# Seven quarter products for the mixture's first layer, in an attention and feed-forward kernel on one Trainium2 core

## The chip, the cores and the metric

The kernel runs on one core of a Trainium2 chip. Its time is that of the device in microseconds, a median over runs. A profile is one execution with an instruction trace.

## The reference

Three layers follow one another on 1152 tokens of 512 features. An attention (2 sequences, 8 heads, 576 tokens, 64 features a head) adds a softmax over pooled groups of four tokens and a local one in a band. Its output x goes through a feed-forward layer of 2048 hidden units, and that through a mixture of four experts of 1024 hidden units each, every expert on every token:

```python
def _moe_ref(x, w_in, w_out, s, b):
    h = x @ w_in
    r = np.maximum(h, 0.0)
    return (s * (r * r) + b) @ w_out

def _moe2_ref(x, domain_probs, w1, w2):
    p = domain_probs / (domain_probs.sum(-1, keepdims=True) + 1e-09)
    out = np.zeros_like(x)
    for e in range(4):
        h = np.maximum(x @ w1[e], 0.0)
        out += p[:, e:e + 1] * (h @ w2[e])
    return out
```

## The kernel before

Each float32 operand of a large product is split into two float32r parts, hi and lo, and a product is made in three passes: hi hi, hi lo, lo hi (`PAIRS`, line 209 in `products`). Activations are stored with features on the partitions: `xs[0]`, `xs[1]` are the hi and lo parts of x, [128, 4, 1152], and `acc` is the float32 sum of a layer's output, in the mixture seen as tokens by features (`acc_t`).

The hidden units are cut into blocks of 512: blocks 0 to 3 are the feed-forward layer, blocks 4 to 11 the mixture, two for each expert. The weights of a block come in four quarters of [128, 1024] (two of the first, two of the second matrix), loaded by `load_next` through SyncE's queue into two rotating `raw` buffers and made ready by `prep` in small steps: for the mixture a ScalarE cast (hi, L174) and a VectorE subtraction (lo, L178). The steps wait in a list, `side`; `side_step` takes one, and the plan calls it between products. The ready parts lie in the pools `wp`, `wx` and `wy`, four places for a half of a first matrix and four for a half of a second.

In the feed-forward layer `moe1_l1` makes 128 hidden units for a group of tokens with 12 products (four 128-row terms by three passes) and then square, scale and split on ScalarE and VectorE (L623 to L636); `moe1_l2` makes 128 output features and adds them to `acc` on VectorE (L651), in the last block also the hi and lo parts of the mixture's x (L653, L654). Groups are of 384 tokens in blocks 1 to 3. In the mixture `moe2_l1` makes 128 hidden units for a part of the tokens: part 0 has 640 tokens, as two pieces of 320 beside each other in two PSUM banks, part 1 has 512. Relu on ScalarE (L680) and a subtraction on VectorE (L681) give hi and lo. `moe2_l2` makes a tile of 128 tokens by 512 features with 12 products and adds it, weighted, on VectorE (L704). PSUM has eight banks: three in `psm`, five in `psx`, handed out by `mm_bank`.

After the attention the order is written as a plan of (time, step) that is sorted: the first layer of a stage stands beside the second layer of a stage before. The feed-forward's last second-layer steps stand beside the mixture's first steps. The plan's order is the order in which instructions are named; a scheduler in the build lays down each engine's queue, by priority in that order among the instructions whose inputs it takes to be there.

## Time and profile before

| | us |
|---|---|
| median of 3 runs | 727.75 (727.34 to 728.23) |
| span of the profiled execution | 727.1 |
| mean granted TensorE clock | 0.969 |
| TensorE busy | 714.3 |
| VectorE busy | 330.9 |
| ScalarE busy | 282.0 |
| GpSimd (POOL) busy | 54.1 |

The span runs from the first to the last instruction; the median is 0.65 us above it. Busy times are shares of the span, and an engine's own waits are not in them. Matmuls are pipelined, so the row of a group gives the length of one from its start to its modelled end, and the distance between two starts is what a product costs in a stream.

### The profile page before, as it was taken

How to read it: one execution, taken by the hardware profiler on the slowest of the kernel's cores; microseconds unless marked ns; L12 is line 12 of the kernel's file. 1: busy time of each engine (PE TensorE's matmuls, PEld its weight loads, DVE VectorE, ACT ScalarE, POOL GpSimd, SP SyncE). 2: the span in 40 equal slices, each digit the busy share in tenths (PEclk: the TensorE clock that was granted, in tenths of full speed). 3: DMA queues.
4: the chain of work that ended last, by engine and by line, in shares of the span. 5: the costliest groups of instructions: out<-in, count | busy, mean ns of one | idle time of the engine just before them, and what ended most of it. 6: DMA issues, size and time to landing. Idle time of an engine off the chain costs nothing.

```text
span 727.1 us, 10493 instructions
## 1 busy us (share of the span) xinstructions
PE 714.3 (98%) x4248; PEld 635.3 (87%) x4248; DVE 330.9 (46%) x573; ACT 282.0 (39%) x662; POOL 54.1 (7%) x62
## 2 busy tenths in 40 slices
PE   6999999999999999999999999999999999999997
PEld 3687888889999999999898898898988988988886
DVE  1468986678893432554213324333333243232222
ACT  2456867668975565733323113122122121120110
POOL 3235244120000000000000000000000000000000
PEclk7559999999999999999999999999999999999999
DMA  6446625533440010211101103003112021000012
GB/s 160 129 112 166 146 42 103 151 103 113 133 145 30 2 57 1 87 30 58 40 20 59 58 1 87 29 1 87 30 57 59 1 60 56 1 1 0 1 44 87
DMA packets 54545, 46.35 MB, mean 64 GB/s; under 512 B 32608, under 2 KB 43104, under 8 KB 54496
## 3 DMA queue, kind: packets, MB, share of 16 engines
q1 hardware_dynamic: 54496, 45.67, 22.9%
q8 instruction: 33, 0.54, 0.3%
q14 instruction: 16, 0.13, 0.1%
HBM read 43.31 MB, written 2.36 MB: 63 GB/s over the span
## 4 chain that ended last, share of the span: by engine, by line
PE 96%; DVE 1%; ACT 1%; SPq 1%; DMA 1%; POOL 0%; issue 0%
PE psx L209 47%; PE psm L209 36%; PE psa L473 3%; PE psa L551 2%; PE psa L485 2%; PE psa L523 2%; PE psa L245 1%; PE psa L544 1%; DMA v<-in_v_dram 1%; ACT pl L459 1%; PE psa L383 1%; PE psa L401 1%; PE psa L464 0%; SPq L320 0%; SPq L332 0%; DVE pl L502 0%
## 5 line engine op out<-in xcount | busy, mean ns | idle before, releaser
L209 PE MATMUL psx<-x,w 128*128 128x320 f32 (+2 forms) x960 | 187.8, 335 | 0.0
L209 PEld LDWEIGHTS psx<-x,w 128*128 128x128 f32 x960 | 161.8, 188 | 11.0
L209 PE MATMUL psm<-x,w 128*128 128x320 f32 (+3 forms) x816 | 159.0, 330 | 0.0
L209 PEld LDWEIGHTS psm<-x,w 128*128 128x128 f32 x816 | 134.1, 189 | 9.4 <-issue 2.3
L209 PE MATMUL psx<-w,h 128*128 128x512 f32 x528 | 126.7, 390 | 0.0
L209 PEld LDWEIGHTS psx<-w,h 128*128 128x128 f32 x528 | 98.4, 188 | 20.0
L680 ACT ACTIVATE h<-psx 128x320 fp32r<-128x320 f32 (+1 forms) x61 | 28.0, 489 | 143.5 <-PE psx L209 143.5
L209 PE MATMUL psm<-w,h 128*128 128x512 f32 x336 | 80.4, 390 | 0.0
L209 PEld LDWEIGHTS psm<-w,h 128*128 128x128 f32 x336 | 62.6, 188 | 12.6
L681 DVE SCALAR_TENSOR_TENSOR h<-psx,h 128x320 fp32r<-128x320 f32 (+1 forms) x61 | 32.3, 553 | 89.4 <-ACT h L680 89.4
L178 DVE TENSOR_TENSOR w<-raw,w 128x1024 fp32r<-128x1024 f32 x32 | 39.1, 1223 | 53.1 <-ACT w L174 53.1
L209 PE MATMUL psx<-h,w 128*128 128x384 f32 (+1 forms) x336 | 61.2, 330 | 0.0
L209 PEld LDWEIGHTS psx<-h,w 128*128 128x128 f32 x336 | 57.5, 188 | 0.0
L174 ACT CAST w<-raw 128x1024 fp32r<-128x1024 f32 x32 | 33.7, 1052 | 60.4 <-PE psx L209 35.6
L209 PE MATMUL psm<-h,w 128*128 128x384 f32 (+2 forms) x288 | 51.5, 320 | 0.0
L704 DVE SCALAR_TENSOR_TENSOR acc<-psx,pr,acc 128x512 f32<-128x512 f32 x39 | 29.3, 750 | 47.5 <-PE psx L209 47.2
L680 ACT ACTIVATE h<-psm 128x320 fp32r<-128x320 f32 (+1 forms) x35 | 16.4, 491 | 88.3 <-PE psm L209 88.3
L209 PEld LDWEIGHTS psm<-h,w 128*128 128x128 f32 x288 | 44.7, 188 | 2.7 <-issue 1.9
L681 DVE SCALAR_TENSOR_TENSOR h<-psm,h 128x320 fp32r<-128x320 f32 (+1 forms) x35 | 18.8, 556 | 55.0 <-ACT h L680 55.0
L704 DVE SCALAR_TENSOR_TENSOR acc<-psm,pr,acc 128x512 f32<-128x512 f32 x24 | 18.0, 751 | 29.2 <-PE psm L209 29.0
L636 DVE TENSOR_TENSOR h<-r,h 128x384 fp32r<-128x384 f32 x36 | 20.0, 555 | 19.7 <-ACT h L635 19.6
L634 ACT ACTIVATE r<-r,b_sb,s_sb 128x384 f32<-128x384 f32 x36 | 25.6, 712 | 0.9
(83 smaller groups left out, 681.4 us busy)
## 6 DMA issues: line engine op xcount, KB each, us to landing
raw<-in_moe_w_dram SPq DMA_DIRECT2D x32, 512.0 KB
raw<-in_moe_w_in_dram SPq DMA_DIRECT2D x8, 1024.0 KB
raw<-in_moe_w_out_dram SPq DMA_DIRECT2D x8, 1024.0 KB
kn<-in_k_dram SPq DMA_DIRECT2D x16, 144.0 KB
v<-in_v_dram SPq DMA_DIRECT2D x8, 288.0 KB
out_dram<-acc SPq DMA_DIRECT2D x9, 256.0 KB
qn<-in_q_dram SPq DMA_DIRECT2D x16, 80.0 KB
vn<-in_v_dram SPq DMA_DIRECT2D x16, 72.0 KB
```

The source lines that it names most:

```text
L174: nc.scalar.copy(parts[0], st["f"] if n < n_moe1 else raw[n, which, half])
L178: nc.vector.tensor_tensor(out=parts[1], in0=f, in1=f32(parts[0]), op=ALU.subtract)
L209: nc.tensor.matmul(o, stat(ps, kk), mov(pm, kk, i), start=c == 0, stop=c == len(terms) - 1)
L473: nc.tensor.matmul(ps[0][:, t * W : t * W + W], qz[:, t].rearrange("p a q -> p (a q)"), kT[:, k0 : k0 + W], start=False, stop=t == m - 1,)
L485: nc.tensor.matmul(pooled[a], qd[o, :], kd[o, :], start=True, stop=True)
L523: nc.tensor.transpose(ps[:W, n : n + width], x, ident[:width, :width])
L551: nc.tensor.matmul(ps[o, t * TQ : t * TQ + TQ], vn[:, t, a], pT[:, i : i + TQ], start=True, stop=True,)
L634: nc.scalar.activation(out=r, in_=r, func=ACTF.Identity, bias=b_sb, scale=s_sb)
L636: nc.vector.tensor_tensor(out=h[1], in0=r, in1=f32(h[0]), op=ALU.subtract)
L680: nc.scalar.activation(out=h[0][:, o : o + m], in_=ps, func=ACTF.Relu)
L681: nc.vector.scalar_tensor_tensor(out=h[1][:, o : o + m], in0=ps, scalar=0.0, in1=f32(h[0][:, o : o + m]), op0=ALU.max, op1=ALU.subtract,)
L704: nc.vector.scalar_tensor_tensor(out=a, in0=ps, scalar=p_e, in1=a, op0=ALU.mult, op1=ALU.add)
```

## The change

The mixture's first layer is computed by the scheme of seven products. A half of a block (256 hidden units) is a 2 by 2 matrix of quarters A11 to A22 (128 hidden units by 256 features), and a part of the tokens a 2 by 2 matrix B11 to B22 (256 features by half of the part's tokens). Seven products of quarters and of sums of quarters (S1 to S4 of the weights, T1 to T4 of x), with six matmuls each, give the four quarters of the hidden units. `step0` to `step3` hold them: three PSUM banks, a, b and c, are summed into by up to three products, and ScalarE copies (`copy`) and VectorE additions (`add`) take what lies in a bank between two of them.

The sums of x are made once, in `x_sums`, on VectorE and ScalarE. The sums of a weight quarter are made by four GpSimd additions (`total` in `prep2`) and split with the quarter itself in three `piece`s of 512, 256 and 1024 elements a partition. Part 0 stays 640 tokens, as halves of 320, part 1 512 as halves of 256; block 3's groups are cut likewise (320, 320, 256, 256). T1's hi and lo parts lie in place of x's own second half of features 0 to 255, which `moe1_l2` therefore no longer writes.

The mixture has a pool of its own, `m2`, opened after the feed-forward's plan has been run through and its pools closed; its tiles wait for the tiles that lay in the same place (`reuse_waits="tile"`). The mixture's first weights are loaded from there on. It holds two places for the sums of a half's first matrix, three for a half's second matrix, two raw buffers and sixteen h tiles. The mixture's second layer uses `psm` alone, the first `psx`. Comments that the change takes out are left away here.

```diff
@@ -61,9 +61,11 @@
 
     const = ctx.enter_context(tc.tile_pool(name="const", bufs=1))
     big = ctx.enter_context(tc.tile_pool(name="big", bufs=1))
-    wp = ctx.enter_context(tc.tile_pool(name="wp", bufs=1))
-    rawp = ctx.enter_context(tc.tile_pool(name="raw", bufs=2))
-    hp = ctx.enter_context(tc.tile_pool(name="hp", bufs=1))
+    m1ctx = ExitStack()
+    wp0 = m1ctx.enter_context(tc.tile_pool(name="wp0", bufs=1))
+    rawp = m1ctx.enter_context(tc.tile_pool(name="raw", bufs=2))
+    hp = m1ctx.enter_context(tc.tile_pool(name="hp", bufs=1))
+    wp1 = m1ctx.enter_context(tc.tile_pool(name="wp1", bufs=1))
     psm = ctx.enter_context(tc.tile_pool(name="psm", bufs=3, space=bass.MemoryType.PSUM))
...
@@ -92,7 +94,7 @@
     pools = {}
 
     def load_next():
-        if not stream:
+        if not stream or (stream[0][0] >= n_moe1 and "m2" not in pools):
...
-        t = rawp.tile([P, 2048], dt, tag="raw", name="raw")[:, : 1024 * m]
+        if n < n_moe1:
+            t = rawp.tile([P, 2048], dt, tag="raw", name="raw")
+        else:
+            t = pools["m2"].tile([P, 1024], dt, tag="raw2", name="raw2", bufs=2)
         nc.sync.dma_start(out=t.rearrange("p (a b) -> p a b", a=src.shape[1]), in_=src)
...
     def prep(n, which, half):
-        """One quarter made ready for the tensor engine, as small steps."""
+
+        if n >= n_moe1:
+            return prep2(n, which, half)
         i = (2 * n + half) % 4
         if i < 3 - which:
-            pool, nb = wp, 3 - which
+            pool, nb = (wp1 if which else wp0), 3 - which
         else:
...
@@ -171,23 +178,102 @@
             )
 
         def high():
-            nc.scalar.copy(parts[0], st["f"] if n < n_moe1 else raw[n, which, half])
+            nc.scalar.copy(parts[0], st["f"])
 
         def low():
-            f = st["f"] if n < n_moe1 else raw[n, which, half]
-            nc.vector.tensor_tensor(out=parts[1], in0=f, in1=f32(parts[0]), op=ALU.subtract)
+            nc.vector.tensor_tensor(
+                out=parts[1], in0=st["f"], in1=f32(parts[0]), op=ALU.subtract
+            )
             load_next()
             ready.add((n, which, half))
 
...
         nonlocal tail
-        if n < n_moe1:
-            steps = [magnitude] + tail[:1] + [clamp] + tail[1:] + [join, sign]
-            tail = [high, low]
-        else:
-            steps = tail + [high, low]
-            tail = []
+        steps = [magnitude] + tail[:1] + [clamp] + tail[1:] + [join, sign]
+        tail = [high, low]
         return steps
...
+    SLOT = {"A11": 0, "A12": 1, "A22": 2, "S1": 3, "S2": 4, "S3": 5, "S4": 6}
+
+    def prep2(n, which, half):
+        m2 = pools["m2"]
+        cols = 1024 if which else 7 * 256
+        parts = [
+            m2.tile([P, cols], F32R, tag=f"v{which}{c}", name=f"v{which}{c}", bufs=2 + which)
+            for c in range(2)
+        ]
+        wt[n, which, half] = parts
+
+        def done():
+            load_next()
+            ready.add((n, which, half))
+
+        if which:
+
+            def high():
+                nc.scalar.copy(parts[0], raw[n, which, half])
+
+            def low():
+                nc.vector.tensor_tensor(
+                    out=parts[1], in0=raw[n, which, half], in1=f32(parts[0]), op=ALU.subtract
+                )
+                done()
+
+            return [high, low]
+
+        sw = m2.tile([P, 4, 2, P], F32, tag="sw", name="sw", bufs=1)
+
+        def quarter(name):
+
+            w = raw[n, which, half].rearrange("p (k f) -> p k f", k=KD)
+            i, k = int(name[1]) - 1, int(name[2]) - 1
+            return w[:, 2 * k : 2 * k + 2, i * P : i * P + P]
+
+        def operand(name):
+            return quarter(name) if name[0] == "A" else sw[:, int(name[1]) - 1]
+
+        def total(out, x, y, op):
+            nc.gpsimd.tensor_tensor(out=operand(out), in0=operand(x), in1=operand(y), op=op)
+
+        def piece(i, c):
+            if i == 0:
+                src, cols = raw[n, which, half].rearrange("p (k f) -> p k f", k=KD)[:, :, :P], (0, 512)
+            elif i == 1:
+                src, cols = quarter("A22"), (512, 768)
+            else:
+                src, cols = sw.rearrange("p s k f -> p (s k) f"), (768, 1792)
+            out, hi = (
+                t[:, cols[0] : cols[1]].rearrange("p (k f) -> p k f", f=P)
+                for t in (parts[c], f32(parts[0]))
+            )
+            if c == 0:
+                nc.scalar.copy(out, src)
+                return
+            nc.vector.tensor_tensor(out=out, in0=src, in1=hi, op=ALU.subtract)
+            if i == 2:
+                done()
+
+        return [
+            lambda: total("S1", "A21", "A22", ALU.add),
+            lambda: piece(0, 0),
+            lambda: total("S2", "S1", "A11", ALU.subtract),
+            lambda: piece(0, 1),
+            lambda: total("S3", "A11", "A21", ALU.subtract),
+            lambda: piece(1, 0),
+            lambda: total("S4", "A12", "S2", ALU.subtract),
+            lambda: piece(1, 1),
+            lambda: piece(2, 0),
+            lambda: piece(2, 1),
+        ]
+
+    def s_ap(n, half, part, name, kk):
+        while (n, 0, half) not in ready:
+            side_step()
+        c0 = SLOT[name] * 256 + kk * P
+        return wt[n, 0, half][part][:, c0 : c0 + P]
...
-    # the queries of two heads in the blocks of a diagonal: one product makes both heads' scores
-    qzs = [const.tile([P, CUT, 2, TQ], F32, name=f"qz{i}") for i in range(2)]
+
+    qzs = [ap1.tile([P, CUT, 2, TQ], F32, name=f"qz{i}") for i in range(2)]
...
     def h_tiles(stage):
+        if "m2" in pools:
+            return [
+                pools["m2"].tile([P, 640], F32R, tag="h", name="h", bufs=16) for _ in range(2)
+            ]
...
+    PARTS = [(0, 320), (640, 256)]
+
     def group(n, g):
         if n == 0:
             return group0(g)
+        if n == n_moe1 - 1:
+            t0, m = PARTS[g // 2]
+            t0 += g % 2 * m
+            return slice(t0, t0 + m), m
         return slice(g * TG, g * TG + TG), TG
+
+    def n_groups(n):
+        return 4 if n == n_moe1 - 1 else NT // TG
...
-        if n == n_moe1 - 1:
+        if n == n_moe1 - 1 and not (dc < 2 and g % 2):
             nc.scalar.copy(xs[0][:, dc, cols], a)
             nc.vector.tensor_tensor(
                 out=xs[1][:, dc, cols], in0=a, in1=f32(xs[0][:, dc, cols]), op=ALU.subtract
             )
...
-    PARTS = [(0, 640, (320, 320)), (640, 512, (512,))]
-
-    def moe2_l1(n, pi, fc, hs):
-        t0, nt, pieces = PARTS[pi]
-        offs = [sum(pieces[:i]) for i in range(len(pieces))]
-        pss = [mm_bank()[:, :m] for m in pieces]
-        products(
-            pss,
-            KD,
-            lambda part, kk: w1_ap(n, part, kk, fc),
-            lambda part, kk, i: xs[part][:, kk, t0 + offs[i] : t0 + offs[i] + pieces[i]],
-        )
-        h = h_tiles(stage_of(n, pi))
-        hs.append(h)
-        for o, m, ps in zip(offs, pieces, pss):
-            nc.scalar.activation(out=h[0][:, o : o + m], in_=ps, func=ACTF.Relu)
+            return (n - 1) * (NT // TG) + g
+        return (n - n_moe1) * 2 + g
+
+
+    xt = {}
+
+    def x_sums(pi):
+        m2 = pools["m2"]
+        t0, m = PARTS[pi]
+        for name in ("T2", "T3", "T4"):
+            xt[name, pi] = [
+                m2.tile([P, 2, m], F32R, tag=f"{name}{pi}{c}", name=f"{name}{pi}{c}", bufs=1)
+                for c in range(2)
+            ]
+        for name, k in (("B11", 0), ("B21", 2)):
+            xt[name, pi] = [x[:, k : k + 2, t0 : t0 + m] for x in xs]
+        for name, k in (("T1", 0), ("B22", 2)):
+            xt[name, pi] = [x[:, k : k + 2, t0 + m : t0 + 2 * m] for x in xs]
+        b11, b21 = acc[:, :2, t0 : t0 + m], acc[:, 2:, t0 : t0 + m]
+        b12, b22 = acc[:, :2, t0 + m : t0 + 2 * m], acc[:, 2:, t0 + m : t0 + 2 * m]
+
+        def total(name, x, y):
+            t = m2.tile([P, 2, PARTS[0][1]], F32, tag="ts", name="ts", bufs=2)[:, :, :m]
+            nc.vector.tensor_tensor(out=t, in0=x, in1=y, op=ALU.subtract)
+            hi, lo = xt[name, pi]
+            nc.scalar.copy(hi, t)
+            nc.vector.tensor_tensor(out=lo, in0=t, in1=f32(hi), op=ALU.subtract)
+            return t
+
+        t1 = total("T1", b12, b11)
+        t2 = total("T2", b22, t1)
+
+        total("T4", b21, t2)
+        total("T3", b22, b12)
+
+    def moe2_l1(n, pi, half, hs):
+
+        t0, m = PARTS[pi]
+        st = {}
+        hs += [h_tiles(n), h_tiles(n)]
+        h1, h2 = hs[-2:]
+        halves = [slice(0, m), slice(m, 2 * m)]
+
+        def bank(name):
+            st[name] = pools["psx"].tile([P, 512], F32, tag="mx", name="psx")[:, :m]
+            return st[name]
+
+        def product(name, w, x, first):
+            ps = bank(name) if first else st[name]
+            terms = [(kk, a, b) for kk in range(2) for a, b in PAIRS]
+            for c, (kk, a, b) in enumerate(terms):
+                nc.tensor.matmul(
+                    ps,
+                    s_ap(n, half, a, w, kk),
+                    xt[x, pi][b][:, kk],
+                    start=first and c == 0,
+                    stop=c == len(terms) - 1,
+                    skip_group_check=True,
+                )
+
+        def copy(name, out):
+            t = pools["m2"].tile([P, 320], F32, tag=out, name=out, bufs=2)[:, :m]
+            st[out] = t
+            nc.scalar.copy(t, st[name])
+
+        def split(h, hf, t):
+            nc.scalar.activation(out=h[0][:, halves[hf]], in_=t, func=ACTF.Relu)
             nc.vector.scalar_tensor_tensor(
-                out=h[1][:, o : o + m],
-                in0=ps,
+                out=h[1][:, halves[hf]],
+                in0=t,
                 scalar=0.0,
-                in1=f32(h[0][:, o : o + m]),
+                in1=f32(h[0][:, halves[hf]]),
                 op0=ALU.max,
                 op1=ALU.subtract,
             )
 
+        def add(name, t, h, hf):
+            nc.vector.tensor_tensor(out=st[t], in0=st[name], in1=st[t], op=ALU.add)
+            split(h, hf, st[t])
+
+
+        def step0():
+            product("a", "A11", "B11", True)
+            copy("a", "r1")
+            product("b", "A12", "B21", True)
+            add("b", "r1", h1, 0)
+
+        def step1():
+            product("a", "S2", "T2", False)
+            copy("a", "r2")
+            product("c", "S1", "T1", True)
+            copy("c", "r5")
+
+        def step2():
+            product("a", "S3", "T3", False)
+            add("a", "r5", h2, 1)
+            product("c", "S4", "B22", False)
+            add("c", "r2", h1, 1)
+
+        def step3():
+            product("a", "A22", "T4", False)
+            split(h2, 0, st["a"])
+
+        return [step0, step1, step2, step3]
+
     def moe2_l2(n, tt, o, hs):
         e = (n - n_moe1) * BLK // FE
-        ps = mm_bank()
+        ps = psm.tile([P, 512], F32, tag="m", name="psm")
...
+        def run(half, i):
+            if i == 0:
+                hidden["steps"] = moe2_l1(n, g, half, hs)
+            hidden["steps"][i]()
+
+        return [lambda half=half, i=i: run(half, i) for half in range(2) for i in range(4)]
 
     def l2_steps(n, g):
         if n < n_moe1:
             return [lambda dc=dc: moe1_l2(n, g, dc, hidden[n, g]) for dc in range(KD)]
-        t0, nt, _ = PARTS[g]
+        t0, m = PARTS[g]
         return [
-            lambda i=i: moe2_l2(n, t0 // P + i, i * P, hidden[n, g]) for i in range(nt // P)
+            lambda i=i: moe2_l2(n, t0 // P + i, i * P, hidden[n, g]) for i in range(2 * m // P)
         ]
 
...
     for n in range(1, n_moe1):
-        plan.append((t0 - 0.5, prepare((n + 1, 0))))
-        plan.append((t0 + 8 + LAG - 0.5, prepare((n + 1, 1))))
-        for g in range(GROUPS1):
+        if n + 1 < n_moe1:
+            plan.append((t0 - 0.5, prepare((n + 1, 0))))
+            plan.append((t0 + 8 + LAG - 0.5, prepare((n + 1, 1))))
+        for g in range(n_groups(n)):
             plan += [(t0 + 2 * i, f) for i, f in enumerate(l1_steps(n, g))]
             plan += [(t0 + 8 + LAG + 2 * i + 1, f) for i, f in enumerate(l2_steps(n, g))]
             t0 += 8
-    t0 += LAG + 2
+
+    def run_plan(plan):
+        plan.sort(key=lambda x: x[0])
+        for i, (_, f) in enumerate(plan):
+            f()
+            if i % 4:
+                side_step()
+
+    run_plan(plan)
+    while side or tail:
+        side_step()
+    m1ctx.close()
+    pools["m2"] = ctx.enter_context(tc.tile_pool(name="m2", bufs=1, reuse_waits="tile"))
+    for pi in range(2):
+        x_sums(pi)
+    load_next()
+    load_next()
+    prepare((n_moe1, 0), (n_moe1, 1))()
+    plan = []
+    t0 = 0
     for n in range(n_moe1, NB):
         if n + 1 < NB:
             plan.append((t0 + 9.5, prepare((n + 1, 0), (n + 1, 1))))
         for g in range(len(PARTS)):
-            plan += [(t0 + 2 * i, f) for i, f in enumerate(l1_steps(n, g))]
+            plan += [(t0 + 1.25 * i, f) for i, f in enumerate(l1_steps(n, g))]
             plan += [(t0 + 10 + 2 * i + 1, f) for i, f in enumerate(l2_steps(n, g))]
             t0 += 10
-    plan.sort(key=lambda x: x[0])
-    for i, (_, f) in enumerate(plan):
-        f()
-        if i % 4:
-            side_step()
+    run_plan(plan)
```

## Rows read from the trace of the kernel before

**Rows 1.** The page's busy times and shares of the span.

```profile
PE 714.3 (98%) x4248; PEld 635.3 (87%) x4248; DVE 330.9 (46%) x573; ACT 282.0 (39%) x662; POOL 54.1 (7%) x62
```

**Rows 2.** Windows: stretch, length, busy of each engine, granted clock, DMA share, GB/s.

```profile
174.00:319.50 145.50, 145.50 (x853) 145.50 (x853) 80.75 (x117) 99.82 (x176) 0.00 (x0) 1.00 0.22 72
319.50:723.10 403.60, 403.60 (x2054) 352.94 (x2052) 131.19 (x192) 78.00 (x135) 0.00 (x0) 1.00 0.12 37
```

**Rows 3.** TensorE in order of time, mixture: start, length, operation, count.

```profile
458.30 5.60 PE L209 MATMUL psx<-w,h 128*128 128x512 f32 x24
463.74 3.68 PE L209 MATMUL psm<-x,w 128*128 128x320 f32 x24
467.26 2.91 PE L209 MATMUL psm<-w,h 128*128 128x512 f32 x12
```

**Rows 4.** TensorE in order of time, end of block 3.

```profile
309.15 6.40 PE L209 MATMUL psx<-h,w 128*128 128x384 f32 x36
315.39 4.32 PE L209 MATMUL psm<-h,w 128*128 128x384 f32 x24
```

**Rows 5.** TensorE in order of time, block 0's second layer beside block 1.

```profile
176.12 1.58 PE L209 MATMUL psx<-h,w 128*128 128x256 f32 x12
177.54 2.28 PE L209 MATMUL psx<-x,w 128*128 128x384 f32 x12
```

**Rows 6.** Groups by shape: busy us, mean ns of one, idle before and releaser.

```profile
L680 ACT ACTIVATE h<-psx 128x320 fp32r<-128x320 f32 x41 | 16.1, 437 | 102.7 <-PE psx L209 102.7
L681 DVE SCALAR_TENSOR_TENSOR h<-psx,h 128x320 fp32r<-128x320 f32 x41 | 18.5, 486 | 66.4 <-ACT h L680 66.4
L635 ACT CAST h<-r 128x384 fp32r<-128x384 f32 x36 | 18.4, 512 | 8.1 <-PE psx L209 7.4
L636 DVE TENSOR_TENSOR h<-r,h 128x384 fp32r<-128x384 f32 x36 | 20.0, 555 | 19.7 <-ACT h L635 19.6
L174 ACT CAST w<-cv 128x1024 fp32r<-128x1024 f32 x16 | 16.7, 1050 | 2.0 <-DVE cv L164 1.8 <-PE psx L209 0.2
L178 DVE TENSOR_TENSOR w<-raw,w 128x1024 fp32r<-128x1024 f32 x32 | 39.1, 1223 | 53.1 <-ACT w L174 53.1
```

**Rows 7.** GpSimd in order of time, end of the attention.

```profile
158.50 1.63 POOL L581 TENSOR_TENSOR x<-xg,x 128x256 fp32r<-128x256 f32 x1 [3.56 <-ACT x L580]
161.83 0.73 POOL L581 TENSOR_TENSOR x<-xg,x 128x256 fp32r<-128x256 f32 x1 [1.70 <-ACT x L580]
```

**Rows 8.** ScalarE in order of time, block 3.

```profile
290.73 0.48 ACT L623 ACTIVATE r<-psm 128x384 f32<-128x384 f32 x1
291.11 1.04 ACT L174 CAST w<-raw 128x1024 fp32r<-128x1024 f32 x1
292.05 0.52 ACT L633 ACTIVATE r<-r 128x384 f32<-128x384 f32 x1
```

**Rows 9.** Window around two weight loads of the mixture.

```profile
441.00:447.00 6.00, 6.00 (x29) 4.95 (x28) 2.65 (x4) 0.60 (x1) 0.00 (x0) 1.00 0.62 178
```

**Rows 10.** VectorE's last instruction, in order of time.

```profile
723.22 0.75 DVE L704 SCALAR_TENSOR_TENSOR acc<-psx,pr,acc 128x512 f32<-128x512 f32 x1 [1.97 <-PE psx L209]
```

**Rows 11.** TensorE's groups by shape from 164.05 to 173.98 us.

```profile
L209 PE MATMUL psm<-x,w 128*128 128x256 f32 x48 | 5.9, 283 | 0.0
L209 PE MATMUL psm<-x,w 128*128 128x384 f32 x24 | 4.3, 335 | 0.0
```

**Rows 12.** Who waited for whom: us in total, times, longest.

```profile
PEld psa L473 <- DVE qz L415: 4.0, 5, 1.5
```

**Rows 13.** VectorE in order of time beside rows 7.

```profile
158.32 1.23 DVE L164 SCALAR_TENSOR_TENSOR cv<-raw,cv 128x1024 int32<-128x1024 int32 x1
```

**Rows 14.** TensorE in order of time, start of the attention.

```profile
14.07 0.76 PE L485 MATMUL psa<-kd,qd 64*80 64x144 f32 x2 [4.85 <-POOL kd L434]
```

**Rows 15.** Windows of the attention, columns as in rows 2.

```profile
12.00:16.00 4.00, 1.93 (x8) 1.21 (x9) 0.30 (x1) 0.47 (x2) 2.02 (x4) 0.50 1.08 289
52.00:56.00 4.00, 4.00 (x22) 3.43 (x20) 2.19 (x5) 3.54 (x10) 0.00 (x0) 0.59 1.00 159
```

More of the change, by code (lines that the diff above doesn't have):

```diff
@@ L713, in l1_steps @@
         hs = hidden[n, g] = []
-        f = moe1_l1 if n < n_moe1 else moe2_l1
-        return [lambda fc=fc: f(n, g, fc, hs) for fc in range(FC)]
+        if n < n_moe1:
+            return [lambda fc=fc: moe1_l1(n, g, fc, hs) for fc in range(FC)]
+        def run(half, i):
[3 more added lines that the diff above has]
+        return [lambda half=half, i=i: run(half, i) for half in range(2) for i in range(4)]
     def l2_steps(n, g):
```

7 lines of the change are left out of this document (2 added, 5 removed).

## The prediction

> **What bounds the kernel now.** I read the page's busy times first, then the windows by stage, then TensorE's instructions in order of time, and last the durations by shape. The page shows TensorE busy 98% of the span and no other engine above half [rows 1]. The windows split that: from 174.00 to 319.50 (blocks 1 to 3) and from 319.50 to 723.10 (the mixture) its busy time is the length of the stretch, at a granted clock of 1.00 (2.4 GHz) [rows 2]. Busy is not yet limiting, so I looked at the distance from one run of products to the next. 24 products of 512 columns take 463.74 - 458.30 = 5.44 us, 226.7 ns each, and 24 of 320 take 467.26 - 463.74 = 3.52 us, 146.7 ns each [rows 3]. In blocks 1 to 3, 36 products of 384 take 315.39 - 309.15 = 6.24 us, 173.3 ns each [rows 4]. As a check: a mixture block before has 96 products of 320, 48 of 512 in the first layer and 108 of 512 in the second, 14.08 + 10.88 + 24.48 = 49.44 us; eight are 395.5 us, three second-layer tiles of block 3 (36 products, 6.2 us) lie in the same window, and 401.7 of its 403.6 us are explained. So there are next to no waits: TensorE's issue of products is the bound, VectorE (131 of 403.6 us) and ScalarE (78) have room, and a product removed there is time removed until something else becomes late.
>
> **Step 1, the products of the mixture's first layer.** A half of a part takes seven quarter products of two 128-row terms by three passes, 42 matmuls, instead of 48 for the same work. Per block: before 96 of 320 and 48 of 512, 24.96 us. After 84 of 320 (part 0) and 84 of 256 (part 1). The mixture has no 256-column products; block 0's second layer has: 12 take 177.54 - 176.12 = 1.42 us, 118.3 ns each, each with its own weight load [rows 5]. So 84 x 0.1467 + 84 x 0.1183 = 12.32 + 9.94 = 22.26 us, a saving of 2.70 us a block, 21.6 us in eight. An eighth fewer multiplications thus bring 10.8%, because the fixed part of a product (about 13 ns by the three widths) is paid 168 times and not 144.
>
> **Step 2, block 3's groups.** 288 products of 384 (49.9 us) become 192 of 320 and 192 of 256: 28.17 + 22.71 = 50.9 us, +1.0 us.
>
> **Step 3, the turn from the first feed-forward to the mixture.** Before, the mixture's first products stood among block 3's last ones, with weights ready. Now its pool lies in the memory of the closed pools, so weights, sums of weights and sums of x all come at the turn. Durations first [rows 6]: a two-input VectorE operation takes 0.555 us for 384 elements and 1.223 for 1024, so about 0.82 for 640 and 0.69 for 512; a ScalarE cast 0.512 and 1.050, so 0.73 and 0.62. One `total` in `x_sums` is subtract, cast, subtract: 0.82 + 0.73 + 0.82 = 2.4 us for part 0, 2.0 for part 1, eight of them 17.5 us. The weights of a half need four POOL additions of 256 elements, 0.73 to 1.63 us each [rows 7], and three casts and three subtractions of 512, 256 and 1024 elements.
> If all this ran behind block 3's last addition in the order in which the code names it, TensorE would stand for 0.4 + 0.4 + 0.4 (last addition, cast, low part), 17.5, and 0.7 for the first weights: 19.4 us. That is the upper bound. But the queues do not hold the written order: `moe1_l1` names L623 and L633 one behind the other, and ScalarE ran a weight cast between them at 291.11 [rows 8]. An operation moves ahead when its engine is otherwise idle and its inputs exist. `x_sums` of part 0 needs groups 0 and 1 alone; behind those come one first-layer product group and eight second-layer ones of 12 x 118.3 ns, 12.8 us, in which VectorE has only eight additions of 0.42 us and six low parts: room for its 9.5 us. The weight quarter needs the slots of the h tiles of group 2, free four product groups (5.7 us) before the end; four additions, a cast and a subtraction take 2.9 + 1.05 + 1.22 = 5.2 us at POOL's short duration and 8.8 at its long one. The load is there long before: from 441 to 447 us 6 x 178 GB/s = 1.07 MB moved, two such quarters [rows 9], and nothing but an old raw slot holds it. So at the turn only part 1's last three sums (4.1 us of VectorE, with ScalarE's casts in between) remain, beside TensorE's first 12.3 us of part 0, which need 6.8 us of VectorE for their own sums and splits, and up to 4.8 for the weights that follow: 15.7 us of VectorE in 12.3 + 1.4. I take 3 us for this, nearer to the row that shows reordering; bounds 0 and 19.4, the upper one with the clock on top (below).
>
> **Step 4, waits inside a half.** Before, a product group left a bank for good. Now bank a receives three groups and bank c two, and each must wait until ScalarE or VectorE has read the last sum out. The reads take 0.437 us (ScalarE, 320) and 0.486 (VectorE, 320), about 0.38 and 0.42 at 256 [rows 6]; the work that hides them is the product in between, 6 x 0.1467 = 0.88 us or 6 x 0.1183 = 0.71. With about 0.2 us to start (the last VectorE addition starts at 723.22, the products end about 723.02 [rows 10]), 0.1 to 0.2 us stay free. Without cover, where the reading engine is held by a weight cast or subtraction of 1.05 to 1.23 us, TensorE waits. Two places a half have no second-layer tile between them: behind `step1` and in front of `step1` or `step3`. Lower bound nothing: from 164.07 to 174.00, with three banks and a VectorE that never rested, 48 products of 256 and 24 of 384 took 9.93 us where 48 x 0.1183 + 24 x 0.1733 is 9.84 [rows 11]. Upper bound: where TensorE had no cover, in the attention, it waited for VectorE five times, 0.8 us on average [rows 12]; once in each of 32 halves is 25.6 us. A block now gives VectorE 26.6 us (28 operations of m columns 12.7, weight pieces 7.1, nine accumulations of 0.75) and ScalarE 17.6 in 46.7 us, far from saturated, so I stay near the lower row and take 4 us, an eighth of a microsecond a half.
>
> **Step 5, the next block's weights.** Their two slots are those of the running block, so a half can be made ready only after part 1 has used the old one. Behind the first half of part 1 stand the other half (42 x 0.1183 = 5.0 us) and three second-layer tiles (8.2 us): 13.1 us of cover for at most 4 x 1.63 + 1.05 + 1.23 = 8.8 us. Cost nothing; if the tiles were pulled forward, cover would be 5.0 and 3.8 us a block exposed. The mixture's second-layer products, its nine tiles and the last store are unchanged.
>
> A rule speaks against POOL here. The row: a 256-element addition on POOL took 1.63 us when it began at 158.50, while VectorE ran a two-input L164 until 159.55, and 0.73 us alone at 161.83 [rows 7, 13]. The Trainium skill, page "SBUF — State Buffer", section "Who interferes with whom", says that a VectorE operation with two SBUF inputs and a POOL operation reading SBUF exclude each other, and whichever comes second waits for all of the other; the trace agrees for POOL as the second, and shows no clear case of the reverse. By the row alone the sum stays as it is; by the rule the additions may also hold VectorE, which is the third rival.
>
> **The sum.** 727.1 (span of the profiled execution) - 21.6 + 1.0 + 3 + 4 = 713.5; the median shown is 0.65 above that span, so 714 us. Without steps 3 and 4 it would be 707.2.
>
> **Rivals.**
> - *The turn stands bare.* `x_sums` of both parts keeps its place ahead of the weight pieces on VectorE, and TensorE idles 19.4 us. For it: the order of the code. Against: rows 8. After 4.85 us of idling ahead of 14.07 us [rows 14] the granted clock was 0.50, and it came back only between 52 and 56 us [rows 15], so the first products would run at 1.2 GHz; I add 3 us, an estimate: half of the first half's 6.2 us a second time. 707.2 + 22.4 + 4 = 733.6, slower; it decides once the turn costs over 18 us.
> - *Step 4 is mis-sized.* A wait of 0.8 us in every second half gives 707.2 + 3 + 12.8 = 723.0; one in every half 735.8, slower. For it: in-order queues and a 1.2 us subtraction in front of a 0.42 us addition. Against: VectorE is little more than half busy, and rows 11.
> - *POOL holds VectorE.* 64 POOL additions of 0.73 us; if a quarter hit a sum that TensorE waits for, +11.7: 725.9. For it: one POOL addition lay until a VectorE operation of two SBUF inputs was done (rows 7 and 13), and the reverse would cost VectorE up to one addition. Against: the rows show POOL as the loser only.
> - *The next weights come late.* Step 5 without the tiles: 7 x 3.8 = 27 us, 741. Against: the tiles have been interleaved evenly so far.
> - *All waits hidden.* 707 to 708.
> That the products themselves don't shrink would need 256 columns to cost over 147 ns, which rows 5 exclude at this clock.
>
> **Chances.** Forecast 0.56, bare turn 0.12, step 4 with every second half 0.12 and with every half 0.05, POOL 0.05, late weights 0.05, all hidden 0.05. The forecast's own range is 708 to 720; the range asked for runs from 706, under the hidden case, to 731, over POOL, the milder step 4 and the bare turn without the clock's 3 us (730.6), and leaves out a wait in every half, the late weights and about half of the bare turn, 0.16 in all. Faster by over 0.2% (under 726.3, about what a measurement of this kernel can tell from no change) 0.75: 0.55 forecast, 0.05 hidden, 0.10 step 4, 0.05 the rest. Within it 0.07; slower 0.18, of which 0.09 is the bare turn and 0.05 step 4.
>
> **What would show it.** Runs of six products, 0.88 us at 320 and 0.71 at 256 from start to start; 84 + 84 of them a block. At the turn, sums of x ahead of the last additions in VectorE's order and a TensorE gap of a few us at most; the first block longer than the others. Later blocks near 46.7 us plus 0.5. The prediction is wrong if the gap at the turn is over 10 us, if the clock falls there, or if each half shows TensorE waiting for ScalarE or VectorE over 0.3 us.

## The result

The changed kernel takes 722.36 us (median of 20 runs, 720.26 to 733.14) beside 728.87 us for the kernel before (20 runs): ratio 0.9904, 95% interval 0.9888 to 0.9921. It is faster by 1.0%, where 1.9% was forecast: 6.5 us of the 13.7. The wide range (706 to 731) held it, the forecast's own range (708 to 720) did not.

Some executions of either kernel take 8 to 20 us longer; the profiled ones of the changed kernel and of two experiments are of that kind (granted clock 0.50 from 60 to 77 us, in the attention), so their rows are read only from block 1 on, and the medians and ranges of the experiments below leave such executions out, as do 722.0 us for the changed kernel and 728.75 for the kernel before.

The page of the second profile of the changed kernel (span 728.4 us) gives the busy times that answer to [rows 1]. There are 288 more products (4536 against 4248), yet TensorE is busy less; VectorE, ScalarE and GpSimd are busy much more.

```profile
PE 710.0 (97%) x4536; PEld 640.0 (88%) x4536; DVE 410.9 (56%) x757; ACT 349.7 (48%) x846; POOL 104.9 (14%) x126
```

The windows have the columns of [rows 2]. They are the gap between block 3 and the mixture, the first products behind it, the rest of the turn, and the mixture from there to the end.

```profile
334.20:337.90 3.70, 0.14 (x2) 0.00 (x0) 3.59 (x7) 2.40 (x5) 0.00 (x0) 0.80 0.00 0
337.90:343.20 5.30, 5.03 (x17) 4.63 (x18) 5.30 (x9) 4.30 (x8) 0.00 (x0) 0.50 0.22 53
343.20:384.00 40.80, 38.50 (x227) 33.48 (x227) 29.32 (x49) 23.53 (x47) 11.36 (x12) 1.00 0.26 84
384.00:724.00 340.00, 340.00 (x1965) 306.27 (x1965) 175.71 (x307) 116.14 (x248) 36.24 (x48) 1.00 0.13 42
```

What [rows 2] did not have stands in the first three: TensorE idle for 3.6 of 3.7 us, then 5.3 us at a granted clock of 0.50 (1.2 GHz), then 2.3 us of idling in 40.8. From 384 on no wait of TensorE is long enough to show.

TensorE in order of time at the turn, then one block of the steady mixture (start, length, operation, count; in brackets the idle time ahead and what ended it). These rows answer to [rows 3 to 5].

```profile
322.66 4.48 PE L295 MATMUL psx<-h,w 128*128 128x256 f32 x36
326.98 4.48 PE L295 MATMUL psm<-h,w 128*128 128x256 f32 x36
331.30 3.04 PE L295 MATMUL psx<-h,w 128*128 128x256 f32 x24
337.93 1.43 PE L811 MATMUL psx<-x,v 128*128 128x320 f32 x4 [3.60 <-ACT v L253]
...
345.81 1.14 PE L811 MATMUL psx<-T,v 128*128 128x320 f32 x6 [0.48 <-ACT r L823]
...
349.99 0.55 PE L811 MATMUL psx<-x,v 128*128 128x320 f32 x2 [1.31 <-ACT v L253]
...
462.86 2.91 PE L295 MATMUL psm<-v,h 128*128 128x512 f32 x12
...
467.82 0.88 PE L811 MATMUL psx<-x,v 128*128 128x256 f32 x6
468.54 2.91 PE L295 MATMUL psm<-v,h 128*128 128x512 f32 x12
...
480.81 1.04 PE L811 MATMUL psx<-T,v 128*128 128x320 f32 x6
481.69 1.04 PE L811 MATMUL psx<-x,v 128*128 128x320 f32 x6
...
510.28 2.91 PE L295 MATMUL psm<-v,h 128*128 128x512 f32 x12
...
718.83 5.60 PE L295 MATMUL psm<-v,h 128*128 128x512 f32 x24
```

Three things can be worked out. Six quarter products take 468.54 - 467.82 = 0.72 us at 256 columns and 481.69 - 480.81 = 0.88 at 320. The same tile comes a block later at 510.28 - 462.86 = 47.42 us, where the forecast's products alone are 22.26 + 24.48 = 46.74. That leaves 0.68 us of waits a block, 5.4 in eight. And the mixture lasts from 337.93 to 718.83 + 24 x 0.2267 = 724.27, 386.34 us; less 8 x 46.74 and less 5.4 there remain 7.0 us that stand near its start. With the gap of 337.93 - (331.30 + 24 x 0.12) = 3.75 us in front of it the turn costs 10.8 us, not 3. A second count agrees: what the products of the mixture stand apart beyond their steady 0.2267, 0.1467 and 0.1183 us adds up to 7.8 us in its first 45 us and to 4.6 in the other 341. The experiments below are compared by this count; 0.6 of each 45 us is the steady part.

VectorE in the same execution around the last additions to `acc` (L751), and GpSimd's first sums of weights.

```profile
321.42 0.49 DVE L751 TENSOR_TENSOR acc<-psx,acc 128x320 f32<-128x320 f32 x1
...
331.50 0.42 DVE L751 TENSOR_TENSOR acc<-psm,acc 128x256 f32<-128x256 f32 x1 [1.01 <-PE psm L295]
332.94 0.42 DVE L751 TENSOR_TENSOR acc<-psx,acc 128x256 f32<-128x256 f32 x1 [1.02 <-PE psx L295]
333.89 0.42 DVE L754 TENSOR_TENSOR x<-acc,x 128x256 fp32r<-128x256 f32 x1 [0.53 <-ACT x L753]
334.37 0.42 DVE L751 TENSOR_TENSOR acc<-psx,acc 128x256 f32<-128x256 f32 x1
334.71 0.81 DVE L783 TENSOR_TENSOR ts<-acc 128x640 f32<-128x640 f32 x1
```

```profile
328.18 1.61 POOL L239 TENSOR_TENSOR sw<-raw 128x256 f32<-128x256 f32 x2 [158.40 <-PE psm L295]
```

The last addition of groups 0 and 1 (the ones of 320 tokens) is done at 321.91; the first sum of x, which needs nothing else that is computed, starts 12.8 us later, directly behind the very last addition, although VectorE stood idle again and again in between, for 0.5 to 1.0 us at a time (the brackets). GpSimd, with an otherwise empty queue, worked in the new pool's memory at 328.18, six microseconds before block 3's products ended. In the built program that first sum of x waits for no semaphore at all, and its buffer lies where a first-layer weight of block 3 lay, which TensorE read last at 316.1. So nothing on the chip held the sum back but its place in VectorE's queue.

ScalarE's queue has the same order, and it sets the end of the gap:

```profile
335.56 0.72 ACT L785 CAST x<-ts 128x640 fp32r<-128x640 f32 x1 [0.27 <-DVE ts L783]
336.63 0.72 ACT L785 CAST T<-ts 128x640 fp32r<-128x640 f32 x1 [0.34 <-DVE ts L783]
337.26 0.92 ACT L253 CAST v<-raw 128x512 fp32r<-128x512 f32 x2
```

The cast of the first weights, for which the mixture's first product waits, stands behind two casts of sums at 337.26, although GpSimd had read the same raw quarter from 328.18 on.

### The profile page after: what moved, and what is told of

The parts are those of the page before. It is cut to its first block, busy times and chain, and to the rows that moved or that the text cites. A ratio compares the mean times of both kernels' runs of the same rounds, so it can differ in the third digit from the quotient of the medians.

```text
span 730.2 us, 11518 instructions
## 1 busy us (share of the span) xinstructions
PE 709.3 (97%) x4536; PEld 639.3 (88%) x4536; DVE 413.0 (57%) x757; ACT 349.7 (48%) x846; POOL 104.7 (14%) x126
## 4 chain that ended last, share of the span: by engine, by line
PE 92%; DVE 4%; ACT 1%; DMA 1%; SPq 1%; issue 0%; POOL 0%
PE psm L295 42%; PE psx L811 24%; PE psx L295 13%; PE psa L559 3%; PE psa L637 2%; PE psa L571 2%; PE psa L609 2%; PE psa L331 1%; PE psa L630 1%; DVE ts L783 1%; PE psa L487 1%; ACT pl L545 1%; DMA v<-in_v_dram 1%; DVE T L786 1%; PE psa L469 1%; DVE h L827 0%
## 5 line engine op out<-in xcount | busy, mean ns | idle before, releaser
L295 PE MATMUL psm<-v,h 128*128 128x512 f32 x864 | 209.3, 391 | 0.8 <-DVE h L827 0.8
L295 PEld LDWEIGHTS psm<-v,h 128*128 128x128 f32 x864 | 158.5, 188 | 31.1 <-DVE h L827 1.2
L811 PE MATMUL psx<-x,v 128*128 128x320 f32 (+1 forms) x768 | 119.9, 298 | 6.1 <-ACT v L253 5.0
L811 PEld LDWEIGHTS psx<-x,v 128*128 128x128 f32 x768 | 110.3, 191 | 9.3 <-ACT v L253 5.5
L811 PE MATMUL psx<-T,v 128*128 128x256 f32 (+1 forms) x576 | 95.5, 301 | 0.7 <-DVE v L255 0.4
L811 PEld LDWEIGHTS psx<-T,v 128*128 128x128 f32 x576 | 83.8, 189 | 6.4 <-ACT r L823 1.0
L295 PE MATMUL psm<-x,w 128*128 128x320 f32 (+2 forms) x420 | 73.0, 323 | 0.0
L295 PEld LDWEIGHTS psm<-x,w 128*128 128x128 f32 x420 | 65.7, 197 | 2.9 <-issue 2.7
L295 PE MATMUL psx<-h,w 128*128 128x384 f32 (+2 forms) x372 | 62.7, 318 | 0.0
L295 PEld LDWEIGHTS psx<-x,w 128*128 128x128 f32 x252 | 40.7, 188 | 0.0
```

Of the source, the lines that this page charges most:

```text
L295: nc.tensor.matmul(o, stat(ps, kk), mov(pm, kk, i), start=c == 0, stop=c == len(terms) - 1)
L811: nc.tensor.matmul(ps, s_ap(n, half, a, w, kk), xt[x, pi][b][:, kk], start=first and c == 0, stop=c == len(terms) - 1, skip_group_check=True,)
```

## The experiments

Three theories of the turn went into the first runs. *Memory*: the build lays down the queues' order as if no instruction that writes into the new pool could start before all tiles of the closed pools are done, so the work stands behind the last additions wherever it is named. *Names*: it stands there because the code names it there. *Volume*: VectorE has too much to do at the turn in any order.

**The changed kernel again.**

> The changed kernel itself once more, to have its turn undisturbed. All theories: 722 us (720.5 to 723.5), about 6.5 us under the kernel before; blocks 1 to 3 in 152 to 153.5 us; some 3.7 us between the end of block 3's products and the first product of the mixture, about 9 us more of waits and of lower clock in the 40 us behind it, 3 to 5 us in the rest of the mixture.

Measured 721.9 us (721.2 to 722.7). Its rows are those above.

**Named early, same memory.** The plan is cut behind block 3's last first-layer step:

```diff
-    run_plan(plan)
+    cut = t0 - 1.5
+    run_plan([p for p in plan if p[0] < cut])
...
     m1ctx.close()
     pools["m2"] = ctx.enter_context(tc.tile_pool(name="m2", bufs=1, reuse_waits="tile"))
-    for pi in range(2):
-        x_sums(pi)
+    x_sums(0)
     load_next()
     load_next()
     prepare((n_moe1, 0), (n_moe1, 1))()
+    run_plan([p for p in plan if p[0] > cut])
+    x_sums(1)
```

> x_sums(0), the two loads and the weight steps are named ahead of block 3's last eight second-layer steps, x_sums(1) behind them; the new pool still lies in the memory of the closed ones. Theory 'memory' (the queues' order is laid down as if nothing of the new pool could start before the last product has released the closed pools, so the work stands behind the last additions wherever the code names it): 720.5 to 723, as the change, gap at the turn 2.5 to 4 us. Theory 'names' (the work stands late because the code names it late): 711 to 714, gap under 0.7 us. Theory 'volume' (VectorE and ScalarE have too much to do at the turn, whatever its order): 720 to 723.

Measured 724.7 us (722.4 to 725.6). That is no gain but 2.7 us more than the changed kernel, and above what any of the theories had. Its VectorE rows show that naming moved the first sum by one addition only:

```profile
335.05 0.82 DVE L783 TENSOR_TENSOR ts<-acc 128x640 f32<-128x640 f32 x1
335.78 0.42 DVE L751 TENSOR_TENSOR acc<-psx,acc 128x256 f32<-128x256 f32 x1
336.11 0.82 DVE L783 TENSOR_TENSOR ts<-acc,ts 128x640 f32<-128x640 f32 x1
```

In the built program this sum, too, waits for no semaphore. The gap was 3.1 us of idling; the waits of the first 45 us grew from 7.8 to 11.3 us, and why was not followed.

**Own memory, named late.** The first layer's weights and raw tiles go to the right end of SBUF, so that their pools can be closed by themselves eight product groups before the end. A new pool, `me`, takes the place; it holds the sums of part 0, the raw quarters and the first layer's ready weights:

```diff
-    wp0 = m1ctx.enter_context(tc.tile_pool(name="wp0", bufs=1))
-    rawp = m1ctx.enter_context(tc.tile_pool(name="raw", bufs=2))
+    r1ctx = ExitStack()
+    wp0 = r1ctx.enter_context(tc.tile_pool(name="wp0", bufs=1, side="right"))
+    rawp = r1ctx.enter_context(tc.tile_pool(name="raw", bufs=2, side="right"))
...
-    run_plan(plan)
+    cut = t0 - 1.5
+    run_plan([p for p in plan if p[0] < cut])
...
+    r1ctx.close()
+    pools["me"] = ctx.enter_context(
+        tc.tile_pool(name="me", bufs=1, side="right", reuse_waits="tile")
+    )
+    run_plan([p for p in plan if p[0] > cut])
     m1ctx.close()
```

> The opposite: everything is named where the change names it, but the sums of part 0, the raw weights and the first layer's weights lie in a pool of their own, in memory that only the first layer's weights, their raw tiles and conversions held, which are done eight product groups before the end. Theory 'memory': 711 to 714, gap under 0.7 us, the first sum on VectorE over 8 us ahead of the last addition. Theory 'names': 721 to 723, as the change. Theory 'volume': 719 to 722.

Measured 718.2 us (717.4 to 720.0; three executions), 3.8 us under the changed kernel. The first sum of x moved ahead of eight additions, and the gap is gone. VectorE and TensorE in this run:

```profile
316.39 0.82 DVE L784 TENSOR_TENSOR ts<-acc 128x640 f32<-128x640 f32 x1
...
327.38 0.41 DVE L752 TENSOR_TENSOR acc<-psx,acc 128x256 f32<-128x256 f32 x1
```

```profile
324.72 2.56 PE L296 MATMUL psx<-h,w 128*128 128x256 f32 x20
327.12 2.80 PE L812 MATMUL psx<-x,v 128*128 128x320 f32 x18
...
332.69 0.86 PE L812 MATMUL psx<-T,v 128*128 128x320 f32 x4 [2.29 <-DVE v L256]
```

The code names the sums where the change names them, and the first runs 11 us ahead of the last addition: *memory* is right about the place, and *names* falls. What rule the scheduler follows inside is inferred from this order. The forecast of 711 to 714 was too low: 8.0 us of waits stand in the first 45, the longest now for a piece of the weights from VectorE, so the time alone would also allow *volume* (719 to 722).

**Both.** As before, with `x_sums(0)`, the loads and the first layer's weight steps named ahead of the last eight second-layer steps.

> Both: own memory and named early. Theories 'memory' and 'names': 710.5 to 713.5, with no gap over 0.7 us at the turn. Theory 'volume': 719 to 722, the waits only stand elsewhere, among block 3's last products.

Measured 716.9 us (716.4 to 719.3), 5.1 us under the changed kernel and between the theories. There is no gap, but there are 6.2 us of waits in the mixture's first 45 us. One thing that is still late there is read from GpSimd and ScalarE:

```profile
257.82 1.46 POOL L240 TENSOR_TENSOR sw<-raw 128x256 f32<-128x256 f32 x2 [97.39 <-PE psx L296]
...
329.88 2.80 POOL L240 TENSOR_TENSOR sw<-raw 128x256 f32<-128x256 f32 x2 [69.09 <-DVE v L256]
```

```profile
333.22 0.74 ACT L824 COPY r<-psx 128x320 f32<-128x320 f32 x2
334.99 1.05 ACT L254 CAST v<-sw 128x1024 fp32r<-128x1024 f32 x1 [1.03 <-POOL sw L240]
```

The first half's sums of weights were begun at 257.82, 67 us ahead of the mixture. The second half's began at 329.88, when VectorE had read the one buffer `sw`, and ScalarE stood for a microsecond at the cast of them.

**What is in the turn.** Four runs take out or move a single part, the first three in the changed kernel as it is. The first leaves the sums of x out; the products take quarters of x in their place.

> The changed kernel without x_sums: the products T1 to T4 take quarters of x as they are, so eight subtract-cast-subtract chains (17.5 us by their durations) are left out and the output is another; everything else stands where it stood. What it tells is how the turn's 13 us divide between the sums of x and the weights. If the sums' volume on VectorE is the whole of it: 709 to 711, gap under 0.7 us. If the place behind the last additions delays the weights as well: a gap of 1.3 to 2.5 us stays, the waits behind it go, 712 to 715.

```diff
...
-        t1 = total("T1", b12, b11)
-        t2 = total("T2", b22, t1)
-        total("T4", b21, t2)
-        total("T3", b22, b12)
```

Measured 717.3 us (715.7 to 717.7), above both forecasts: a little under 5 us of the turn are the sums of x. A gap of 1.5 us stays, and one wait of 2.83 us, behind ScalarE's cast of the second half's sums of weights:

```profile
335.68 9.54 PE L803 MATMUL psx<-x,v 128*128 128x320 f32 x59 [2.83 <-ACT r L815]
```

So the sums are about half of the turn, and 4.4 us of the other half are these two waits for the weights. Without the sums both their volume and their place are gone, so this run does not tell those two apart.

The second run leaves out GpSimd's sums of weights; the third piece is cast from the raw quarter.

```diff
-                src, cols = sw.rearrange("p s k f -> p (s k) f"), (768, 1792)
+                src, cols = raw[n, which, half].rearrange("p (k f) -> p k f", f=P), (768, 1792)
...
-            lambda: total("S1", "A21", "A22", ALU.add),
...
```

> The changed kernel without the four sums of weight quarters on GpSimd in each half of a block (64 instructions left out, the third piece is cast from the raw quarter instead, so the output is another). If GpSimd's additions hold VectorE, or come too late: 714 to 718, and the mixture behind its first 45 us loses most of its 4.6 us of small waits. If they run beside it unseen: 720.5 to 722.5, the small waits stay, and the turn gains at most 1.5 us (the second half's sums).

Measured 724.2 us (721.3 to 724.9): no gain at all with GpSimd empty, but 1.7 us more than either forecast allowed, with 1.4 us more of waits at the turn, which were not followed. The gap (3.75 us) and the small waits of the steady mixture (5.1 us for 4.6) stay. That GpSimd's additions hold the kernel up falls, at the amount that this kernel has of them.

The third run fills the gap with two products of block 3, made a second time.

```diff
+    n, g = n_moe1 - 1, n_groups(n_moe1 - 1) - 1
+    for dc in range(2):
+        products(
+            [mm_bank()[:, :256]],
+            FC,
+            lambda part, fc: w2_ap(n, part, fc, dc * P, P),
+            lambda part, fc, i: hidden[n, g][fc][0][part],
+        )
     m1ctx.close()
```

> The changed kernel with two second-layer products of block 3 made a second time behind the last one (24 products of 256 columns, 2.8 us, nobody reads them): TensorE works through most of the 3.8 us gap. If the lower clock behind the gap (0.50 for some 5 us, so about 2.5 us) comes from the gap: clock 1.00 at the first products of the mixture, 719 to 720.5. But if the products there wait for VectorE anyway, the clock given back is waited away: 721 to 722.5. If the added products only lengthen the path: 724 to 725.

Measured 721.4 us (720.9 to 722.7), 0.6 us less. The granted clock stays at 1.00 from 328 to 338, and TensorE waits three times for VectorE's pieces of the weights instead (1.12, 0.78 and 0.98 us); the window below has the clock in the third column from the right:

```profile
329.50:336.00 6.50, 4.20 (x23) 3.42 (x24) 6.50 (x11) 4.30 (x9) 0.39 (x1) 1.00 0.20 72
```

```profile
322.79 5.32 PE L295 MATMUL psx<-h,w 128*128 128x256 f32 x43
329.57 0.56 PE L811 MATMUL psx<-x,v 128*128 128x320 f32 x2 [1.47 <-ACT v L253]
331.25 1.73 PE L811 MATMUL psx<-x,v 128*128 128x320 f32 x10 [1.12 <-DVE v L255]
```

The lower clock was a companion of the gap and hardly a cost of its own: 5.3 us had run at half the speed, yet at 1.00 the mixture lasts only 0.5 us less (385.8 for 386.3 us). It also starts later, 4.5 us behind block 3's last own product where it was 3.75.

The fourth run is made from the one with own memory and early names. GpSimd makes the first subtraction of each sum of x, and `sw` has two buffers, a change that is also run alone below.

> The version with its own memory and early names, and two things more that take work and a wait off VectorE's way at the turn: the first subtraction of each of the eight sums of x is made on GpSimd (5.8 us less of VectorE at 0.82 and 0.68 us each), and the sums of weights have two buffers, so the second half's four need not wait for the first half's last piece. If VectorE's crowding (busy without a break from 314.8 to 336 in that version's profile) is what is left at the turn: 713 to 715, waits of the first 45 us of the mixture down from 6.2 to 2 to 3 us. If GpSimd's additions hold VectorE up: no better than 716 to 718. If the left-over comes from the order of TensorE's products: 716.5 to 717.5.

```diff
-            nc.vector.tensor_tensor(out=t, in0=x, in1=y, op=ALU.subtract)
+            nc.gpsimd.tensor_tensor(out=t, in0=x, in1=y, op=ALU.subtract)
```

A miss: 723.1 us (721.9 to 724.0), 6 us above the version it was made from and 7.5 above that version with the two buffers alone. GpSimd and VectorE show why:

```profile
327.83 1.59 POOL L784 TENSOR_TENSOR ts<-acc,ts 128x640 f32<-128x640 f32 x1 [1.69 <-DVE x L787]
329.38 1.33 POOL L240 TENSOR_TENSOR sw<-raw 128x256 f32<-128x256 f32 x1
330.67 1.75 POOL L784 TENSOR_TENSOR ts<-acc 128x640 f32<-128x640 f32 x1
```

```profile
327.98 2.12 DVE L787 TENSOR_TENSOR T<-ts,T 128x640 fp32r<-128x640 f32 x1
330.91 1.79 DVE L755 TENSOR_TENSOR x<-acc,x 128x256 fp32r<-128x256 f32 x1
```

The sums of weights now stand between sums of x in GpSimd's queue. The first begins 7.3 us ahead of the mixture's first product (336.68 here); with the two buffers alone all eight were done 11 us ahead of it (314.4 of 325.7). So the weights come late again. And VectorE's subtractions stretch from 0.82 to 2.12 and from 0.42 to 1.79 us while GpSimd works on an operation of its own.

**The two waits that were left.** Two buffers for `sw`, and `x_sums(1)` named behind the first half of part 0:

```diff
-        sw = m2.tile([P, 4, 2, P], F32, tag="sw", name="sw", bufs=1)
+        sw = m2.tile([P, 4, 2, P], F32, tag="sw", name="sw", bufs=2)
...
-    x_sums(1)
     prepare((n_moe1, 1))()
-    plan = []
+    plan = [(4.5, lambda: x_sums(1))]
```

> The version with its own memory and early names (e4_both, 716.9), and one thing more: two buffers for the sums of weights. There, GpSimd's four sums for the second half begin only when the first half's last piece is read (329.88, behind VectorE), and ScalarE's cast of them waits with two reads of finished banks queued behind it. If this is a term of its own: 713.5 to 715.5, GpSimd's first eight sums all long before the turn, waits of the mixture's first 45 us 3 to 4.5 us where e4_both has 6.2. If VectorE's crowding alone holds the turn: 716 to 717.5.

With the buffers alone, on the version with own memory and early names: 715.6 us (715.1 to 716.0), 1.3 under it, with 4.8 us of waits in the first 45. It is a term of its own, but a smaller one than expected.

> The same with two buffers for the sums of weights, and x_sums(1), which the mixture needs only 12 us later, named behind the first half of part 0 instead of ahead of it, so that VectorE's eight operations of it no longer stand in front of the additions that TensorE waits for. If VectorE's order is what is left: 711.5 to 714, first 45 us under 3 us of waits. If the volume in those 30 us is what is left, the waits move to part 1: 713.5 to 716, about as e9_two_sw.

With both: 715.1 us (713.4 to 715.5), by the medians 1.8% under the kernel before (728.5 in the same series) and 1.0% under the changed kernel. Its TensorE rows at the turn:

```profile
322.73 3.04 PE L296 MATMUL psx<-h,w 128*128 128x256 f32 x24
325.61 1.99 PE L812 MATMUL psx<-x,v 128*128 128x320 f32 x12
327.63 0.56 PE L812 MATMUL psx<-T,v 128*128 128x320 f32 x2
...
338.19 0.86 PE L812 MATMUL psx<-T,v 128*128 128x320 f32 x4 [0.35 <-DVE v L256]
```

Block 3 ends at 322.73 + 24 x 0.12 = 325.61, where the mixture begins; the waits of the first 45 us are 2.8 us, 0.6 of which every 45 us of the mixture have. By the waits, VectorE's order was what was left. The times alone do not show it: they hardly part from those of the buffers alone, and 715.1 lies above this theory's 711.5 to 714 and inside the other's 713.5 to 716. The profiled execution is the fastest of the five; what keeps the others near 715 was not followed.

> The changed kernel with two buffers for the sums of weights, and nothing else. The wait of 1.3 us at 350 us in its profile (for ScalarE's cast of the second half's sums) should go, and with it 1 to 2 us of the turn: 719.5 to 721. If the cast is late for VectorE's sake and not for the buffer's: 721.5 to 722.5.

The buffers on the changed kernel itself: 721.3 us (719.7 to 721.8), between its two forecasts. The wait of 1.3 us at 350 us is gone, the gap (4.0 us here) is not.

**Step 4 by itself.** No second-layer tile among the first layer's products:

```diff
-            plan += [(t0 + 10 + 2 * i + 1, f) for i, f in enumerate(l2_steps(n, g))]
+            plan += [(t0 + 9.6 + 0.01 * i, f) for i, f in enumerate(l2_steps(n, g))]
```

> The changed kernel with all second-layer tiles of a part behind its first-layer steps, none among the first-layer steps of the next part. It takes from the halves the cover that the tiles give. By step 4 (cover by the product in between is nearly enough, an eighth of a us a half): the small waits of the mixture behind its first 45 us stay near 4.6 us, up to 7; 721 to 725. If the tiles were the cover: a wait of 0.2 to 0.4 us more in each of 28 halves, 728 to 734.

Measured 721.9 us (721.0 to 722.6), as the changed kernel. The first-layer products of part 0 now stand in runs of 84, and hold their pace:

```profile
479.70 1.04 PE L811 MATMUL psx<-T,v 128*128 128x320 f32 x6
480.58 1.04 PE L811 MATMUL psx<-x,v 128*128 128x320 f32 x6
481.46 1.04 PE L811 MATMUL psx<-T,v 128*128 128x320 f32 x6
```

0.88 us for six, with a bank's sum read out behind each: the product in between is cover enough, and the tiles are not needed for it.

## Why the prediction was wrong

**Step 1, right.** Six products were forecast at 0.88 and 0.71 us and measured at 0.88 and 0.72; -21.6 us stands.

**Step 2, right.** Products of 256 columns came 4.32 / 36 = 0.120 us apart (326.98 less 322.66, where the 36 before these begin) instead of 0.118: +1.3 us for +1.0.

**Step 3, the step that failed: its overlap.** It was right that weights, sums of weights and sums of x all come at the turn, and GpSimd found its place in memory free early (328.18), as it said. It was wrong that the sums of part 0 run beside block 3's last 12.8 us. They stood behind its last addition, and the turn cost 10.8 us where the sum has 3. The prediction took from [rows 8] that an operation moves ahead when its engine is idle and its inputs exist. In [rows 8] the weight cast wrote to a pool that was long open. The sums write to a pool opened in the place of closed ones, and in the order that the build lays down they stand behind everything that used those. The prediction asked when the place comes free on the chip, and did not ask what the scheduler takes to be free.

Four kernels, with and without own memory and early names, show it: 722.0 as changed, 724.7 with early names, 718.2 with own memory, 716.9 with both. Naming alone gains nothing; memory alone takes the whole gap. The gap and the waits of the first 45 us together are 11.6, 14.6, 8.0 and 6.2 us. What is left lies in two terms that step 3 priced low or not at all: the second half's weights, held by the one `sw` buffer, which it did not name (6.2 to 4.8 us with two), and VectorE's crowd, which it did see (4.8 to 2.8 with `x_sums(1)` later; in the times this last gain is not clear). The prediction had also named a fall of the clock at the turn as a sign of being wrong, and the clock fell.

**Step 4, right.** It had 4 us for what TensorE waits inside the halves. Measured are 0.68 us a block, 5.4 in eight, of which the kernel before had some 2 us of its own in the same stretch (401.7 of 403.6 explained). That is near the lower row, as chosen.

**Step 5, right.** From 384 us on no wait for weights shows.

The sum again with the measured terms: -21.6 + 1.3 + 10.8 + 5.4 less the 2 that were there before is -6.1 us; the medians differ by 6.5. In the last version of the turn, where it costs about 2 us, the kernel comes to 713.4 to 715.5; the prediction had put it at 714 with 3 us for the turn.

**The rivals.** *The turn stands bare* did half of what it said: the order was the order of the code, but TensorE idled 3.75 us and not 19.4, since it needs only the first half's weights to start; the clock fell as it said, to 0.50 for about 5 us, and cost little, because at 1.00 the products wait for VectorE. *POOL holds VectorE* falls in the time: without GpSimd's sums nothing is gained. Its mechanism exists all the same (below). *Step 4 is mis-sized* and *the next weights come late* did not happen.

## What to carry to other kernels

Where work is to move ahead of a stage's end, it is not enough that its inputs and its memory are free in time on the chip: the queue's order is fixed in the build, and a pool opened in the place of closed pools can put its writers behind the last users of those, wherever the code names them. Give the work that crosses a stage's boundary memory that comes free earlier, in a pool of its own, and look at the next profile for idle time on the engine ahead of the work. Then look for the next thing in line: a single buffer between two halves, and operations needed late that stand in a queue ahead of some needed now.

## What the runs showed of the hardware

GpSimd and VectorE exclude each other in these rows, and VectorE can be the one that waits, which [rows 7, 13] had not shown. In the run with sums of x on GpSimd, a VectorE subtraction of 640 elements that began at 327.98 ended at 330.10; at its usual 0.82 us (as at 326.86, with GpSimd idle) it would have ended at 328.80. The GpSimd operation that had begun 0.15 us ahead of it ended at 329.42, 0.68 us before it. The Trainium skill, page "SBUF — State Buffer", section "Who interferes with whom", has it as a lock, where whichever comes second waits for all of the other; the trace agrees, now in both directions. GpSimd's 64 additions in 386 us cost this kernel nothing that can be measured. Eight longer operations in its most crowded 30 us went with a loss of 7.5 us; how much of it was this exclusion and how much the order in GpSimd's queue was not separated.

A lower granted clock need not cost much: with 5.3 us at 0.50 the mixture lasted 0.5 us longer than with none, for TensorE at 1.00 waited most of the difference away.
